# A fused recurrent-attention and MLP kernel: the second-layer weights loaded in fp32 by the common queue and cast on the chip, with the later order reworked

## The chip, the cores and the metric

The kernel runs on one core of one Trainium2 chip. The core has a matrix engine (TensorE, PE in the profile), a vector engine (VectorE, DVE), a scalar engine (ScalarE, ACT), a general engine (GpSimd, POOL) and SyncE (SP), which here only issues DMAs. Sixteen DMA engines move the data of all queues. The metric is the device time of one execution in microseconds, the median of several runs; lower is better.

## The reference

The inputs are r, k, v of shape (4, 8, 768, 48), that is batch, heads, time steps and head size, then w and u (8, 48), a norm's gain g_ln (384) and the weights w_ch1 (384, 1536) and w_ch2 (1536, 384), all in fp32.

```python
state = zeros(B, H, D, D)
for t in range(S):
    cur = einsum('bhd,bhe->bhde', u * k[t], v[t])
    y[t] = einsum('bhd,bhde->bhe', r[t], state + cur)
    state = w * state + einsum('bhd,bhe->bhde', k[t], v[t])
x = y as (B, S, H * D)
xn = (x - mean(x)) / sqrt(var(x) + 1e-6) * g_ln
out = x + maximum(xn @ w_ch1, 0) @ w_ch2
```

## The kernel before, in words

**Tiling.** The 4 x 768 time steps are cut into 24 chunks of 128 steps, six to a batch. Within a chunk the recurrence is done as matrix products: scaled k (`sk`) and scaled r (`sr`) are transposed, multiplied with each other and masked (`A`), and the sum of A times v and of the carried state `Z` times r is the chunk's y. Chunks 0 to 3 are worked on in another layout, with step names that end in 2. The MLP works on groups of chunks: chunks 0 to 7 and 20 to 23 are groups of one, chunks 8 to 19 are groups of two (`GROUPS`, line 14).

**Order.** The order is written out by hand in the string `PLAN` (lines 18 to 66). Each word is a step: its name, its index, and its engine (v VectorE, s ScalarE, g GpSimd, - for steps with one fixed engine, and for a DMA the queue of SP). The kernel issues the steps in that order (line 754), and each engine takes its own steps strictly in that order; semaphores make an engine wait where a step needs the result of another engine or a buffer that is still read. So a step that waits holds back everything behind it on its engine, and a DMA that waits on SP holds back all later DMAs of SP.

**Steps.** These are the ones that matter here; i is a chunk, g a pair of chunks.

- `LK`, `LR`, `LV` and `LK2`, `LR2`, `LV2` load k, r, v on SP (lines 350 to 376). They read pieces of 48 fp32 numbers.
- `LW1,kc` loads a third of w_ch1 (128 rows of 1536 fp32) into the tile `w1_f[kc]`. `SW,i` multiplies a 128 x 512 piece of it by the gain and casts it to bf16, into `w1_sb[n][kc]` with n = i // 3 and kc = i % 3.
- `IW2,n` loads a third of w_ch2 by a DMA on GpSimd's queue that casts from fp32 to bf16 as it moves the data, into `w2_sb[n]` (line 348).
- `SK`, `SR`, `SR2` scale k and r; `TRk`, `TRr` transpose them on TensorE, `TCk`, `TCr` copy the result out of PSUM; from chunk 8 on (for r from chunk 18 on) `TDk`, `TDr` do both by a transposing DMA on SP. `Q2` multiplies the transposed k and r; `AT`, `AT2` are the products, `AM`, `AM2` the masks.
- `CV2,g` casts the v of two chunks to bf16. `S,i` adds the outer products of chunk i to the state in PSUM, and for an even i first forms the diagonal terms, which `CC2` copies out and `VB2` multiplies by v. `ZU` and `ZD` finish the state.
- `Y,i` and `Y2,i` are y in PSUM; `X,i` adds the `VB2` part and gives x with its row sum; `SQ` is the sum of squares, `RS` the reciprocal root, `XN` the centred x in bf16. `LT` and `XT` transpose xn by TensorE and a copy; from group 8 on `LTD` does it by a transposing DMA on SP.
- `UP,16*g+m` is a piece of the first layer for group g (512 hidden columns in 12 matmuls for a group of one, 256 in 6 wider ones for a group of two), into one of two PSUM buffers that `Y2` uses as well; `RL` applies the maximum with 0 and frees that buffer. m runs over 0 to 2 for a group of one, and then needs the `SW` with n = m.
- `DN,4*i+d` is a third of the second layer for chunk i, reading `w2_sb[d]`. `OT,i` scales by `RS` and adds x, `STO` stores. `DU` are matmuls on zeros without use for the result.

The names that the profile prints are those of the program, with the digits of buffers left out: `w_sb` stands for the tiles of both weights, `hp` for the two PSUM buffers of `UP` and `Y2`, `y` for that of `S` and `Y`, `o` for that of `DN`, `at` for that of transposes and `AT`.

Of the kernel before, what the change touches and what calls it, by code (L numbers as in the profile page):

```python
# [29 lines left out]
DN,2,- Q2,3,g CV2,3,g RS,0,g S,6,- CC2,3,s RS,2,g RL,48,s VB2,3,g UP,50,- OT,0,v LR2,5,- LR2,6,- LK,8,- LK,9,- LK,12,- LK,11,-  # L30
LK,10,- SR2,5,g SK,9,g SR2,4,v ZU,6,v AM,6,v DN,4,- LT,4,- DN,5,- DN,6,- XT,4,s RL,50,s UP,49,- OT,1,v SK,8,v LT,5,- TRr,4,-
UP,65,- TCr,4,v XT,5,s RL,49,s RL,65,s RS,4,g SK,12,g SQ,3,s RS,3,s DN,8,- Y,6,- X,6,v XN,6,v DN,9,- DN,10,- S,7,- LT,6,-
UP,66,- OT,2,v ZU,7,v SR2,6,v DN,12,- Y,7,- DN,13,- DN,14,- RL,66,v OT,3,v XT,6,s UP,82,- RL,82,s UP,64,- TDk,4,- LV,8,- LV,9,-
LK,13,- AT,8,- AT,9,- RS,5,g ZD,7,g Q2,4,g SK,11,g STO,0,- STO,2,- LV,13,- LR2,7,- LV,10,- SK,10,v TDk,5,- LV,11,- X,7,v RL,64,s
CV2,4,s XN,7,s AM,8,v AM,9,v UP,98,- UP,97,- DN,16,- RL,98,s UP,80,- S,8,- DN,17,- TRr,5,- ZU,8,v SK,13,g CC2,4,s RL,97,s SQ,6,s
DN,18,- S,9,- LT,7,- RL,80,s OT,4,v ZD,8,v ZU,9,v VB2,4,g UP,81,- RL,81,v XT,7,s TCr,5,s DN,20,- TRr,6,- Y,9,- UP,96,- Q2,5,v
X,9,v STO,1,- LK,17,- LK,16,- TDk,6,- UP,113,- Y,8,- DN,21,- DN,22,- X,8,v ZD,9,v XN,8,v XN,9,g TCr,6,s CV2,5,s SQ,8,s S,10,-
ZU,10,v ZD,10,g SK,17,v OT,5,v CC2,5,v RL,113,s RL,96,s SQ,7,s AT,10,- AT,11,- UP,114,- UP,112,- SR2,7,v AM,11,v VB2,5,g RS,6,g
RS,7,g SK,16,g DN,24,- DN,25,- DN,26,- RL,112,s RL,114,s AM,10,v Y,11,- X,11,v OT,6,v LTD,8,- UP,133,- UP,128,- RL,133,v STO,3,-
LV,14,- LK,14,- LV,12,- LK,15,- LR2,8,- LR,18,- AT,13,- AT,12,- Y,10,- Q2,6,v X,10,v RL,128,s SQ,9,s RS,8,g AM,12,v SK,14,v  # L40
DN,28,- UP,129,- UP,131,- DN,29,- XN,10,s XN,11,s RL,129,s RL,131,s CV2,6,g DN,30,- S,12,- UP,130,- UP,132,- AM,13,v OT,7,v
SK,15,v LTD,9,- LV,15,- TDk,7,- STO,4,- LR,19,- STO,5,- LK,19,- CC2,6,s RL,130,s RL,132,s DN,32,- TRr,7,- ZU,12,v Y,13,- VB2,6,v
X,13,v XN,13,g UP,146,- DN,33,- TCr,7,v RL,146,s Y,12,- UP,144,- CV2,7,v UP,148,- DN,34,- RL,148,s RL,144,s SQ,11,s X,12,v
S,13,- Q2,7,v OT,8,v XN,12,g SR2,8,g AT,14,- AT,15,- UP,149,- DN,36,- LTD,10,- LV,16,- LV,17,- TDk,8,- LR,21,- LK,18,- LK,20,-
STO,7,- STO,6,- ZU,13,v ZD,13,v S,14,- AM,15,v SQ,12,s RL,149,s DN,37,- DN,38,- UP,147,- SQ,13,s SQ,10,s CC2,7,v ZU,14,v
RL,147,s ZD,14,g AM,14,v VB2,7,g SR,18,g SK,19,g UP,161,- S,15,- ZU,15,v RL,161,s TRr,8,- UP,163,- UP,145,- RL,163,s TCr,8,s
CV2,8,s RS,9,g Y,15,- OT,9,v RL,145,v X,15,v UP,164,- UP,160,- Y,14,- X,14,v XN,14,g SK,18,g ZD,15,g SR,19,v Q2,8,v DN,44,-
AT,17,- AT,16,- XN,15,s RL,160,s RL,164,s LTD,11,- UP,162,- DN,45,- DN,46,- S,16,- RL,162,s CC2,8,s SQ,15,s RS,10,s AM,16,v
OT,11,v LV,18,- TDk,9,- TDr,9,- STO,8,- UP,165,- ZU,16,v VB2,8,v DN,40,- DN,41,- DN,42,- RL,165,s SQ,14,s RS,11,s LV,19,-
SK,20,g Q2,9,g OT,10,v ZD,16,v Y,16,- UP,180,- RL,180,s AM,17,v X,16,v XN,16,v DN,48,- UP,177,- DN,49,- UP,176,- DN,50,-  # L50
RL,176,s Y,17,- OT,12,v AT,19,- AT,18,- X,17,v UP,178,- DN,52,- XN,17,s CV2,9,v AM,18,v S,18,- DN,53,- SQ,17,s CC2,9,s RL,178,s
RL,177,s VB2,9,g DN,54,- ZU,18,v STO,9,- LR,20,- OT,13,v SR,20,g SR,21,g LK,21,- STO,12,- LTD,12,- STO,11,- STO,10,- UP,179,-
RL,179,s Y,18,- UP,181,- DN,56,- DN,57,- UP,194,- AM,19,v RL,181,v DN,58,- X,18,v UP,193,- Y,19,- LV,20,- LV,21,- TDr,10,-
OT,14,v X,19,v XN,18,v XN,19,v SQ,18,s RL,193,s RL,194,v DN,60,- UP,197,- S,19,- DN,61,- UP,192,- SQ,16,s RS,12,s RL,197,s
SQ,19,s ZU,19,v CV2,10,v RL,192,v SK,21,g TDk,10,- Q2,10,g DN,62,- UP,195,- UP,196,- RL,195,s RL,196,s OT,15,v ZD,19,v AT,21,-
AT,20,- AM,20,v AM,21,v LTD,13,- LK,23,- LK,22,- LR,22,- LR,23,- SK,23,g SK,22,g SR,22,g STO,13,- TDk,11,- STO,14,- SR,23,g
TDr,11,- Q2,11,g DN,64,- DN,65,- UP,208,- S,20,- UP,210,- DN,66,- ZU,20,v RL,208,s CC2,10,s RL,210,s UP,212,- Y,20,- RL,212,s
OT,16,v UP,209,- DN,68,- DN,69,- VB2,10,v X,20,v RL,209,v ZD,20,v UP,213,- DN,70,- OT,17,v UP,211,- Y,21,- RS,13,s XN,20,s
RL,213,s RL,211,s LV,22,- LTD,14,- LV,23,- DN,72,- DN,73,- AT,23,- AT,22,- X,21,v S,21,- DN,74,- AM,23,v ZU,21,v OT,18,v
CV2,11,g UP,224,- UP,225,- DN,76,- SQ,21,s XN,21,s SQ,20,s RL,225,s LTD,15,- STO,16,- STO,15,- S,22,- ZD,21,g AM,22,v CC2,11,v  # L60
ZU,22,v VB2,11,g UP,240,- DN,77,- RL,240,s RS,15,s RL,224,s Y,22,- DN,78,- UP,242,- UP,226,- X,22,v ZD,22,v OT,19,v XN,22,s
RS,14,g RL,226,s RL,242,v DN,80,- Y,23,- X,23,v DN,81,- DN,82,- UP,241,- LTD,16,- UP,257,- OT,20,v RL,241,s RL,257,s DN,84,-
# [724 lines left out]
```

## Time and profile before

| | us |
|---|---|
| median of 3 runs | 153.11 (152.23 to 153.35) |
| the profiled execution | 151.87 |
| its span, first to last instruction | 150.1 |
| TensorE busy, of the span | 140.2 (93%) |
| VectorE, ScalarE, GpSimd busy | 112.8, 82.3, 87.7 |

The profile is of one execution. A line such as `L650 PE MATMUL hp<-xT,w_sb ... x648 | 57.7, 240 | 0.5 <-DVE` says: line 650, on TensorE, matmuls that read xT and w_sb and write hp, 648 of them, 57.7 us busy in all, 240 ns for one on average, and 0.5 us in which TensorE had waited ahead of them for VectorE. A row of the waits such as `PE y L485 <- POOL vv L394: 2.7, 1, 2.7` gives the engine that waited with its line, the one it waited for, us in total, how often, and the longest. Matmuls overlap, so the time of one step is better read from the chain of waits, where rows follow each other in time (start, length, what). SPq and POOLq are the issuing of DMAs.

### The profile page before, as it was taken

To read this page: it belongs to the slowest core of one execution; us is meant where nothing else is said; L and a number is where in the kernel's file an instruction comes from. 1 tells how busy PE (TensorE), PEld (TensorE's weight loads), DVE (VectorE), ACT (ScalarE), POOL (GpSimd) and SP (SyncE) were. 2 spreads that over 40 slices of the span, in tenths; PEclk is the share of its full clock that TensorE was granted. 3 is DMA by queue.
4 is the path that set the end of the run, shared out by engine and by line. 5 is a ranking of instruction groups with operands and counts; after the bars stand their busy time and mean duration, and the time that the engine had idled before them with its cause. 6 is when DMAs were issued, how large, how long until landed. Compare 5 with 4: busy or idle time off the path is not lost.

```text
span 150.1 us, 4669 instructions
## 1 busy us (share of the span) xinstructions
PE 140.2 (93%) x1936; PEld 112.4 (75%) x1936; DVE 112.8 (75%) x195; ACT 82.3 (55%) x181; POOL 87.7 (58%) x107
## 2 busy tenths in 40 slices
PE   7998798669999899999999999999999999999991
...
GB/s 117 298 240 327 258 364 223 223 236 207 186 129 24 213 216 215 168 129 177 231 146 202 160 213 168 142 207 207 210 162 177 190 155 161 135 24 38 158 144 66
DMA packets 84329, 27.18 MB, mean 181 GB/s; under 512 B 80338, under 2 KB 83540, under 8 KB 84308
## 3 DMA queue, kind: packets, MB, share of 16 engines
...
q10 hardware_dynamic: 2, 0.00, 0.0%
...
## 4 chain that ended last, share of the span: by engine, by line
PE 68%; SPq 12%; DMA 10%; POOL 4%; DVE 2%; issue 1%; ACT 0%; POOLq 0%; ACTq 0%
PE hp L650 29%; PE o L678 25%; DMA vf<-in_v_dram 7%; SPq L334 3%; DMA xT<-xn 3%; PE at L548 3%; SPq L351 2%; PE y L587 2%; SPq L373 2%; PE y L485 2%; SPq L376 2%; PE y L579 2%; POOL Vb L496 1%; POOL sr L204 1%; PE at L404 1%; SPq L370 1%
## 5 line engine op out<-in xcount | busy, mean ns | idle before, releaser
L650 PE MATMUL hp<-xT,w_sb 128*128 128x128 bf16 (+1 forms) x648 | 57.7, 240 | 0.5 <-DVE w_sb L343 0.4
L650 PEld LDWEIGHTS <-w_sb 128*128 128x128 bf16 x648 | 49.8, 115 | 4.2 <-DVE w_sb L343 0.5
L678 PE MATMUL o<-w_sb,hT 128*128 128x384 bf16 x276 | 52.8, 326 | 0.0
L666 ACT ACTIVATE hT<-hp 128x512 bf16<-128x512 f32 x55 | 32.1, 596 | 35.6 <-PE hp L650 35.0
L678 PEld LDWEIGHTS <-hT 128*128 128x128 bf16 x276 | 25.1, 98 | 11.9
L557 DVE TENSOR_TENSOR A<-at,mask 128x1024 bf16<-128x1024 f32 x20 | 24.0, 1213 | 1.1 <-PE at L548 1.1
L734 DVE SCALAR_TENSOR_TENSOR ot<-o,rs,x 128x384 f32<-128x384 f32 x23 | 14.1, 614 | 9.3 <-PE o L678 7.5
L496 POOL TENSOR_TENSOR Vb<-vf,cc 128x768 f32<-128x768 f32 x9 | 14.8, 1642 | 6.7 <-ACT cc L199 6.0
L204 POOL TENSOR_TENSOR q<-trk,trr 128x1024 bf16<-128x1024 bf16 x5 | 10.7, 2131 | 13.6 <-DMA trk<-sk 4.9
L204 POOL TENSOR_TENSOR sk<-kf,Fk 128x384 bf16<-128x384 f32 (+1 forms) x15 | 16.4, 1103 | 0.9 <-DMA kf<-in_k_dram 0.9
L204 POOL TENSOR_TENSOR sr<-rf,Fr 128x384 bf16<-128x384 f32 (+1 forms) x11 | 16.1, 1477 | 1.1 <-ACT Fr L297 1.0
L594 DVE SCALAR_TENSOR_TENSOR x<-y,Vb 128x384 f32<-128x384 f32 x20 | 11.0, 551 | 7.3 <-PE y L587 6.0
L601 ACT ACTIVATE sqj<-x,sm 128x384 bf16<-128x384 f32 x24 | 14.7, 610 | 3.4 <-DVE x L594 3.2
L668 DVE TENSOR_SCALAR hT<-hp 128x512 bf16<-128x512 f32 x17 | 11.5, 685 | 3.9 <-PE hp L650 3.9
L610 POOL TENSOR_SCALAR xn<-x,sm 128x384 bf16<-128x384 f32 x8 | 5.7, 716 | 12.3 <-DVE x L594 12.1
L485 PE MATMUL y<-vv,sk 128*128 128x96 bf16 (+1 forms) x96 | 7.5, 207 | 2.7 <-POOL vv L394 2.7
L204 POOL TENSOR_TENSOR Z<-ZS,WLZ 128x384 bf16<-128x384 f32 x5 | 5.9, 1183 | 5.0 <-DVE ZS L569 5.0
L278 PE MATMUL o<-warm 128*128 128x512 bf16 x26 | 7.7, 437 | 1.0 <-DVE warm L227 1.0
L485 PEld LDWEIGHTS <-sk 128*128 128x128 bf16 (+1 forms) x96 | 5.3, 97 | 4.3 <-issue 3.7
L204 DVE TENSOR_TENSOR sk<-kf,Fk 128x384 bf16<-128x384 f32 x8 | 5.9, 752 | 3.1 <-ACT Fk L300 3.1
L199 ACT COPY trr<-at 128x512 bf16<-128x512 bf16 (+1 forms) x11 | 7.7, 774 | 0.4 <-PE at L404 0.4
L620 POOL TENSOR_SCALAR rs<-sq 128x1 f32<-128x1 f32 (+1 forms) x10 | 1.9, 193 | 10.2 <-ACT sqj L601 9.6
...
## 6 DMA issues: line engine op xcount, KB each, us to landing
out_dram<-ot SPq DMA_DIRECT2D x23, 192.0 KB, 3.3
kf<-in_k_dram SPq DMA_DIRECT2D x20, 192.0 KB, 4.7
vf<-in_v_dram SPq DMA_DIRECT2D x20, 192.0 KB, 3.7
rf<-in_r_dram SPq DMA_DIRECT2D x9, 384.0 KB, 4.6
w_f<-in_moe_w_ch_dram SPq DMA_DIRECT2D x3, 768.0 KB, 6.9
w_sb<-in_moe_w_ch_dram POOLq DMA_DIRECT2D x3, 384.0 KB, 6.9
rf<-in_r_dram SPq DMA_DIRECT2D x6, 192.0 KB, 3.5
kf<-in_k_dram SPq DMA_DIRECT2D x2, 384.0 KB, 4.4
```

The source lines that it names most:

```text
L199: nc.scalar.copy(out=out, in_=in_)
L204: engines[e].tensor_tensor(out=out, in0=in0, in1=in1, op=ALU.mult)
L485: nc.tensor.matmul(out=t[:, q * E2 : (q + 1) * E2].rearrange("p (e d) -> p e d", e=2), lhsT=lhs, rhs=rhs, start=first, stop=True, skip_gro ...
L496: engines[e].tensor_tensor(out=Vb2(g).rearrange("p (x h d) -> p x h d", x=2, h=H), in0=vals, in1=cc2(g)[:].unsqueeze(3).to_broadcast([P, 2 ...
L557: nc.vector.tensor_tensor(out=AA(i)[:].rearrange("p e q t -> p (e q) t"), in0=psum["at", i][:].rearrange("p e q t -> p (e q) t"), in1=mask ...
L594: nc.vector.scalar_tensor_tensor(out=xx(i)[:], in0=psum["y", i][:, :C], scalar=1.0, in1=Vb(i), op0=ALU.mult, op1=ALU.add, accum_out=sm[i][:],)
L601: nc.scalar.activation(out=sqj[:], in_=xx(i)[:], func=ACT.Square, bias=sm[i][:], scale=-float(C), accum_out=sq[g][:, j : j + 1])
L650: nc.tensor.matmul(out=t[:, a * gw : (a + 1) * gw], lhsT=w1_sb[n][kc][:, fb::FB], rhs=xT(g)[:, :size, kc, :], start=(kc == 0), stop=(kc == ...
L666: nc.scalar.activation(out=o, in_=s, func=ACT.Relu)
L668: nc.vector.tensor_relu(out=o, in_=s)
L678: nc.tensor.matmul(out=psum["o", i][:, :C], lhsT=hT(g)[:, fk, j * P : (j + 1) * P], rhs=w2_sb[d][:, a, :], start=(fk == 0), stop=(fk == FK ...
L734: nc.vector.scalar_tensor_tensor(out=ot(i)[:], in0=psum["o", i][:, :C], scalar=rs[g][:, j : j + 1], in1=xx(i)[:], op0=ALU.mult, op1=ALU.add,)
```

## The change

The three casting loads `IW2` on GpSimd's queue are gone. `LW2,n` on SP's queue reads the same third of w_ch2 as fp32 into `w1_f[n]`, the tile that held a third of w_ch1; so it must wait until `SW` n, n + 3 and n + 6 have read that tile. Six steps `CW2,i` cast half a third each (128 x 768) to bf16, three on GpSimd (0, 2 and 5) and three on ScalarE (1, 3 and 4); `w2_sb` is cut into halves accordingly, and `DN` picks the half. The three fp32 tiles get another name, nothing else changes in them. `LW2` stands in the order behind `LV,4` and `LV,5`, ahead of `LV,7`, `LV,6` and all later loads.

From line 23 on the order of the steps is another one, and 106 steps that are in both versions run on another engine. Among them, `SW` stands four times on GpSimd, four times on ScalarE and once on VectorE (before: two, six and one), `XN` twelve times on GpSimd (before: eight), `Q2` always on VectorE (before: five of twelve on GpSimd). The matmuls are the same.

```diff
--- before
+++ after
@@ the order, from line 23 @@
-SR2,3,g VB2,0,g SR2,2,g AT2,1,- TRk,1,- S,1,- FR,0,s TCk,1,s CV2,1,s UGC,0,s AM2,1,v Y2,1,- TRr,3,- Y2,0,- Q2,1,v TCr,3,s ZU,1,v
-X,0,v AT2,3,- LK,6,- LV,5,- LV,4,- S,2,- AM2,3,v ZU,2,v AT2,2,- AM2,2,v SW,6,s CC2,1,s XN,0,g MP,4,g SK,5,g TRr,2,- TCr,2,s
-VB2,1,g SW,3,g IW2,0,g IW2,1,g SK,7,g DU,1024,- S,3,- X,1,v XN,1,v TRk,2,- TCk,2,s LT,0,- Y2,2,- AT,4,- XT,0,v X,2,v AM,4,v
-SW,2,g SW,8,v LR2,4,- LV,6,- LV,7,- SW,7,s SW,1,s SW,4,s AT,5,- Y2,3,- DU,512,- LT,1,- UP,2,- X,3,v CV2,2,g SK,6,v XN,3,g XN,2,g
-IW2,2,g SW,5,s RL,2,v XT,1,s UP,17,- SQ,0,s SW,0,s RL,17,s Q2,2,v ZU,3,v TRk,3,- UP,0,- UP,18,- S,4,- AM,5,v TCk,3,s RL,0,s
-UP,16,- LT,2,- RL,18,v LT,3,- UP,1,- CC2,2,s RL,16,s XT,2,v UP,33,- RL,33,s SQ,1,s RL,1,s VB2,2,g ZU,4,v XT,3,v Y,5,- X,5,v
-DN,0,- UP,34,- Y,4,- X,4,v RL,34,v UP,32,- AT,7,- AT,6,- RS,1,s SQ,4,s SQ,2,s SQ,5,s XN,4,s RL,32,v XN,5,v AM,7,v DN,1,- UP,48,-
...
+SR2,3,g VB2,0,g AT2,1,- TRk,1,- S,1,- FR,0,s TCk,1,s AM2,1,v Y2,1,- LK,6,- LV,4,- LV,5,- TRr,3,- Y2,0,- TCr,3,s CV2,1,g ZU,1,v
+Q2,1,v X,1,v SR2,2,v AT2,3,- S,2,- AM2,3,v TRr,2,- SQ,1,s TCr,2,s CC2,1,v ZU,2,v X,0,v AT2,2,- DU,1024,- S,3,- AM2,2,v MP,4,g
+XN,1,g SK,5,g VB2,1,g TRk,2,- XN,0,s LT,0,- UGC,0,s SW,6,s XT,0,s ZU,3,v TCk,2,v Y2,2,- LT,1,- AT,4,- Y2,3,- X,2,v AM,4,v SW,8,v
+SW,7,s XT,1,s SW,3,s SW,4,s SK,7,g SW,0,g XN,2,g DU,512,- AT,5,- LT,2,- UP,2,- SW,5,g SW,2,g SW,1,g X,3,v XN,3,v XT,2,v RL,2,s
+UP,18,- LT,3,- SK,6,v XT,3,v Q2,2,v AM,5,v RL,18,s UP,1,- TRk,3,- UP,0,- RL,1,s TCk,3,s RL,0,v UP,50,- SQ,0,s LW2,0,- CV2,2,g
+S,4,- CC2,2,s VB2,2,g CW2,0,g UP,48,- CW2,1,s RL,50,s RL,48,s LW2,2,- CW2,5,g AT,6,- AT,7,- ZU,4,v Y,5,- X,5,v XN,5,v AM,6,v
+UP,33,- UP,16,- SQ,2,s RL,16,s RL,33,s LW2,1,- LV,7,- LV,6,- CW2,3,s CW2,4,s LK,9,- LK,11,- LR2,4,- LR2,5,- LK,8,- LV,9,-
+LR2,6,- LV,10,- Y,4,- CW2,2,g DN,0,- UP,32,- UP,17,- RL,32,s DN,1,- DN,2,- CV2,3,g RS,0,s Q2,3,v X,4,v LT,5,- AM,7,v OT,0,v
+SR2,4,g RS,2,g XN,4,g S,6,- UP,49,- RS,1,s CC2,3,s RL,17,v VB2,3,v SQ,4,s XT,5,s DN,4,- UP,80,- RL,80,s SQ,3,s RL,49,s DN,5,-
+DN,6,- ZU,6,v SK,9,v UP,81,- RL,81,v OT,1,v UP,34,- TRr,4,- Y,7,- RL,34,v X,7,v RS,4,s TCr,4,s DN,8,- LT,4,- XT,4,s DN,9,-
+DN,10,- S,7,- UP,65,- SK,8,g TDk,4,- LV,8,- LK,10,- LK,14,- LV,13,- LR2,7,- STO,0,- LV,11,- ZU,7,v OT,2,v SR2,5,g TRr,5,-
...
+Y,9,- DN,18,- TRr,6,- VB2,4,g UP,113,- AM,8,v X,9,v OT,4,v S,9,- ZU,9,v LT,6,- DN,20,- Y,8,- DN,21,- UP,112,- DN,22,- X,8,v
+XT,6,v XN,9,g SR2,7,g TDk,5,- LV,16,- CV2,5,g XN,8,g RL,113,s SQ,5,s TCr,6,s SQ,9,s RS,5,s Q2,5,v RL,112,s UP,97,- RL,97,s
+AT,11,- AT,10,- UP,96,- STO,1,- STO,2,- LK,13,- OT,5,v LK,12,- SK,13,g LTD,8,- LK,15,- LV,12,- UP,114,- S,10,- ZD,9,v SK,12,v
+TDk,6,- AM,11,v ZU,10,v CC2,5,v ZD,10,v RL,96,s UP,98,- DN,24,- SQ,6,s RL,114,s RL,98,s RS,6,s UP,131,- AM,10,v RL,131,v
...
@@ -185,9 +185,9 @@
     g_neg = const.tile([P, CK], FP32, name="g_neg")
     WLZ = const.tile([P, HP, E2], FP32, name="WLZ")
     uwI = const.tile([P, HP, 2], BF16, name="uwI")
-    w1_f = [const.tile([P, F], FP32, name=f"w1_f{kc}") for kc in range(CK)]
+    w1_f = [const.tile([P, F], FP32, name=f"w_f{kc}") for kc in range(CK)]
     w1_sb = [[const.tile([P, FW], BF16, name=f"w1_sb{n}_{kc}") for kc in range(CK)] for n in range(NW)]
-    w2_sb = [const.tile([P, FK // NW, C], BF16, name=f"w2_sb{n}") for n in range(NW)]
+    w2_sb = [[const.tile([P, FB // 2, C], BF16, name=f"w2_sb{n}_{a}") for a in range(2)] for n in range(NW)]
     w1_src = moe_w_ch1.rearrange("(kc p) f -> p kc f", p=P)
     w2_src = moe_w_ch2.rearrange("(n p fk) c -> p n fk c", p=P, n=NW)
 
@@ -344,8 +344,16 @@
         else:
             nc.gpsimd.tensor_scalar(out=o, in0=s, scalar1=g, scalar2=1.0, op0=ALU.mult, op1=ALU.mult)
 
-    def IW2(n, e):
-        nc.gpsimd.dma_start(out=w2_sb[n][:], in_=w2_src[:, n])
+    def LW2(n, e):
+        queues[e].dma_start(out=w1_f[n][:].rearrange("p (k c) -> p k c", k=FB), in_=w2_src[:, n])
+
+    def CW2(i, e):
+        n, a = divmod(i, 2)
+        o, s = w2_sb[n][a][:].rearrange("p k c -> p (k c)"), w1_f[n][:, a * F // 2 : (a + 1) * F // 2]
+        if e == "g":
+            nc.gpsimd.tensor_scalar(out=o, in0=s, scalar1=1.0, scalar2=1.0, op0=ALU.mult, op1=ALU.mult)
+        else:
+            copy(e, o, s)
 
     def LK(i, e):
         queues[e].dma_start(out=kf(i), in_=chunk_src(k, i))
@@ -678,7 +686,7 @@
             nc.tensor.matmul(
                 out=psum["o", i][:, :C],
                 lhsT=hT(g)[:, fk, j * P : (j + 1) * P],
-                rhs=w2_sb[d][:, a, :],
+                rhs=w2_sb[d][2 * a // FB][:, a % (FB // 2), :],
                 start=(fk == 0),
                 stop=(fk == FK - 1),
             )
@@ -693,7 +701,7 @@
             nc.tensor.matmul(
                 out=psum[name][:, : C // 2],
                 lhsT=hT(g)[:, fk, j * P : (j + 1) * P],
-                rhs=w2_sb[i][:, a, c0 : c0 + C // 2],
+                rhs=w2_sb[i][2 * a // FB][:, a % (FB // 2), c0 : c0 + C // 2],
                 start=(fk == 0),
                 stop=(fk == FK - 1),
             )
@@ -745,7 +753,7 @@
 
     steps = dict(
         MW=MW, MO=MO, ML=ML, MZ=MZ, MI=MI, MI2=MI2, MM=MM, MM2=MM2, MP=MP, TL=TL, DU=DU, WF=WF, UF=UF, LG=LG, UGC=UGC,
-        LN=LN, WBM=WBM, FK=FK_, FR=FR_, FK2=FK2, FR2=FR2, UWR=UWR, COL=COL, UW=UW, WL=WL, LW1=LW1, SW=SW, IW2=IW2,
+        LN=LN, WBM=WBM, FK=FK_, FR=FR_, FK2=FK2, FR2=FR2, UWR=UWR, COL=COL, UW=UW, WL=WL, LW1=LW1, SW=SW, LW2=LW2, CW2=CW2,
         LK=LK, LR=LR, LV=LV, LK2=LK2, LR2=LR2, LV2=LV2, SK=SK, SR=SR, SK2=SK2, SR2=SR2, SKH=SKH, SRH=SRH, CV2=CV2,
         TRk=TRk, TRr=TRr, TCk=TCk, TCr=TCr, TDk=TDk, TDr=TDr, Q2=Q2, AT2=AT2, AT=AT, AM2=AM2, AM=AM, S=S_, CC2=CC2,
         ZU=ZU, ZD=ZD, VB2=VB2, Y2=Y2, Y=Y, X=X, SQ=SQ, XN=XN, RS=RS, LT=LT, LTD=LTD, XT=XT, UP=UP, RL=RL, DN=DN,
```

64 lines of the change are left out of this document (28 added, 36 removed).

## The prediction

> **What bounds the kernel now.** I read the page first (shares, and the span in 40 slices), then PE's own waits, then busy times by stretch, then the chain of waits back from the stall.
>
> ```profile
> PE 140.2 (93%) x1936; PEld 112.4 (75%) x1936; DVE 112.8 (75%) x195; ACT 82.3 (55%) x181; POOL 87.7 (58%) x107
> ...
> PE   7998798669999899999999999999999999999991
> ```
>
> TensorE is busy for 93% of the span, and its missing 9.9 us lie almost wholly in the first 14 slices and the last. Its waits, from 28 us on:
>
> ```profile
> PE y L485 <- POOL vv L394: 2.7, 1, 2.7
> PE at L635 <- DVE xn L610: 0.7, 1, 0.7
> ```
>
> The busy times by stretch (length, then busy us with count of PE, PEld, DVE, ACT, POOL; then granted clock, DMA share, GB/s):
>
> ```profile
> 28.75:31.51 2.76, 0.01 (x2) 0.00 (x1) 0.74 (x2) 0.00 (x0) 0.89 (x2) 0.95 1.16 270
> 31.25:34.66 3.41, 3.15 (x32) 3.15 (x31) 1.04 (x3) 0.77 (x2) 3.38 (x6) 0.50 0.98 212
> ```
>
> ```profile
> 65.00:70.00 5.00, 4.85 (x71) 3.79 (x69) 4.78 (x7) 2.57 (x6) 3.97 (x4) 1.00 0.61 130
> ...
> 80.00:100.00 20.00, 20.00 (x238) 16.48 (x235) 17.08 (x29) 13.32 (x32) 12.16 (x13) 1.00 0.89 191
> 100.00:120.00 20.00, 20.00 (x221) 16.08 (x220) 17.15 (x28) 9.39 (x23) 11.87 (x10) 1.00 0.97 186
> ```
>
> Late in the kernel TensorE never pauses, so only fewer matmuls or an earlier start help there. The one large hole is 28.75 to 31.51, behind which the granted clock stands at 0.50 for 3.41 us. The chain of waits (start, us) says who made the hole:
>
> ```profile
> 20.10 10.37 DMA vf<-in_v_dram
> ...
> 30.62 0.84 POOL vv L394
> ...
> 31.51 0.48 PE y L485 x4
> ...
> 36.03 0.65 PE o L678 x4
> 36.69 0.67 PE hp L650 x12
> ...
> 41.04 0.18 PE y L464 x8
> ```
>
> The second v load of chunks 4 and 5 is issued at 20.10 and lands 10.37 us later; GpSimd casts it (CV2,2), and only then can S,4 go on. (The rows at 36 us are one DN, 0.65, and one UP, 0.67; S,6 begins at 41.04.) The issues around it:
>
> ```profile
> 19.42 4.19 SPq L357 DMA_DIRECT2D vf<-in_v_dram  x2
> 22.47 1.34 POOL L348 DMA_DIRECT2D w_sb<-in_moe_w_ch_dram  x2
> ```
>
> ```profile
> w_sb<-in_moe_w_ch_dram POOLq DMA_DIRECT2D x1, 384.0 KB, 5.3
> vf<-in_v_dram SPq DMA_DIRECT2D x1, 192.0 KB, 10.4
> ```
>
> (The second pair is the DMA view for 22.4 to 23.2 us, the last number being us to landing.) The first casting weight load starts at 22.47, over 2 us after that v load, and is down at about 27.8, 2.7 us before it. So the weight loads on GpSimd's queue pass the v load that the next matmul needs.
>
> **The change, part by part.**
>
> *The weight loads move (IW2 gone, three LW2 in).* LW2 stands on SP's queue behind LV,4 and LV,5, so it cannot pass them. Without the overtaking I give the second load twice the usual landing:
>
> ```profile
> w_f<-in_moe_w_ch_dram SPq DMA_DIRECT2D x3, 768.0 KB, 6.9
> ...
> xT<-xn SPq DMA_TRANSPOSE x10, 2.8
> ```
>
> ```profile
> L357 SPq DMA_DIRECT2D vf<-in_v_dram x20: 428/610/3505, 19.4 to 125.1; - x20
> ...
> DMA to landing us min/median/max: 3.1/3.7/10.4
> ```
>
> 20.10 + 7.4 = 27.5. CV2,2 costs GpSimd 0.83 (below) and S,4 now has five UP ahead of it, so the stall goes: 2.75 us. The half clock behind it goes too: 3.15 us of work done at clock 0.50 is 1.6 us lost. Together -4.35. What GpSimd spent on issuing (three times about 0.6) goes as well, off the path.
>
> *The order before the first UP.* In the old order UP,2 waits for SW,8 on VectorE (its row of the timeline, then groups of VectorE by shape: xn, Z, sr, three copies):
>
> ```profile
> 24.24 0.89 DVE L343 TENSOR_SCALAR w_sb<-w_f,g_neg 128x512 bf16<-128x512 f32 x1
> ```
>
> ```profile
> L610 DVE TENSOR_SCALAR xn<-x,sm 128x384 bf16<-128x384 f32 x7 | 5.7, 832 | 0.1
> ...
> L204 DVE TENSOR_TENSOR Z<-y,WLZ 128x384 bf16<-128x384 f32 x8 | 4.4, 547 | 0.8 <-PE y L485 0.8
> ...
> L204 DVE TENSOR_TENSOR sr<-rf,Fr 128x768 bf16<-128x768 f32 x3 | 3.1, 1021 | 0.0
> ...
> L201 DVE COPY xT<-at 128x384 bf16<-128x384 bf16 x3 | 1.1, 350 | 4.1 <-PE at L635 4.1
> ...
> L201 DVE COPY trr<-at 128x1024 bf16<-128x1024 bf16 x1 | 0.7, 692 | 0.5 <-PE at L404 0.5
> ...
> L201 DVE COPY cc<-y 128x16 f32<-128x16 f32 x3 | 0.5, 165 | 0.2 <-PE y L485 0.2
> ```
>
> Between Q2,1 and SW,8 VectorE gains SR2,2 (1.02), ZU,3 (0.55), TCk,2 (0.69) and CC2,1 (0.17), and loses ZU,1 (0.55, now ahead of Q2,1), XN,1 (0.83) and XT,0 (0.35): 2.43 - 1.73 = +0.70. With 0.1 for its waits on x, SW,8 ends at about 25.9, not 25.1, and I charge +0.8. Bounds: 0, if VectorE's old small waits absorb it; +1.8, if SR2,2 doubles beside GpSimd.
>
> *SP's new waits.* LW2,n overwrites the fp32 W1 tile n, so SP waits for SW n, n+3 and n+6. Four SW are now on GpSimd, and there XN,2 waits for X,2 (VectorE, about 24.0), then come SW,5, SW,2, SW,1 (groups by shape, and the Vb rows' shortest, median and longest):
>
> ```profile
> L666 ACT ACTIVATE hT<-hp 128x512 bf16<-128x512 f32 x55 | 32.1, 596 | 35.6 <-PE hp L650 35.0
> ...
> L610 POOL TENSOR_SCALAR xn<-x,sm 128x384 bf16<-128x384 f32 x8 | 5.7, 716 | 12.3 <-DVE x L594 12.1
> ...
> L199 ACT CAST vv<-vf 128x768 bf16<-128x768 f32 x5 | 4.2, 838 | 1.0 <-DMA vf<-in_v_dram 1.0
> ...
> L341 ACT ACTIVATE w_sb<-w_f,g_neg 128x512 bf16<-128x512 f32 x6 | 4.0, 715 | 0.0
> ...
> L394 POOL TENSOR_SCALAR vv<-vf 128x768 bf16<-128x768 f32 x4 | 3.3, 831 | 5.8 <-DMA vf<-in_v_dram 5.7
> ...
> L345 POOL TENSOR_SCALAR w_sb<-w_f,g_neg 128x512 bf16<-128x512 f32 x2 | 1.7, 835 | 0.0
> ```
>
> ```profile
> L496 POOL TENSOR_TENSOR Vb<-vf,cc x9: 1476/1480/2228, 14.7 to 130.8; 128x768 f32<-128x768 f32 x9
> ```
>
> 24.0 + 0.72 + 3 x 0.835 = 27.2 for SW,1. X,2 stands one mask step ahead of SW,8, hence 24.0. LW2,0 can go when ScalarE has done SW,3 (about 24.9: X,0 at 21.0, then XN,0, three SW at 0.715 and two XT), LW2,2 at 26.4, LW2,1 at 27.2. By the W1 loads' 6.9 us they land at 31.8, 33.3 and 34.1. Queued behind them on SP are LV,7, LV,6 and all later loads: issued by about 29.3, landed by 33 (3.7) to 36.7 (the last weight load's 34.1 and one v load's worth more). Their reader CV2,3 comes on GpSimd after the casts, at 35.2, and S,6 wants it at 37.8: hidden, up to +0.5 at the bad end.
>
> *Six casts.* Three on ScalarE at 0.838, three on GpSimd at 0.831, same shape as CV2. TensorE: UP,2 from 25.95, five UP at 0.67, LT,3 and TRk,3 0.8 (S,4 at 30.1, until 30.85), then UP,48, AT,6, AT,7 and Y,5 1.6, UP,33 at 32.45, UP,16, Y,4, and DN,0 at 34.2, DN,1 at 36.2. GpSimd: CC2,2 follows S,4 at about 31.1, then VB2,2 1.48 (32.6), CW2,0 (33.5), CW2,5 (34.3), CW2,2 (35.2): 0.7 ahead of DN,0 and 1.0 ahead of DN,1, covered by S,4, UP and Y. Without cover, all four steps longer by half (2228 against 1476), the chain ends at 37.1 and costs 0.95. On ScalarE CW2,1 stands behind CC2,2, and behind it RL,50, which frees the PSUM buffer for UP,33: with LW2,0 down by 31.1 it is 31.15 + 0.84 + 0.6 = 32.6, 0.15 late; with LW2,0 at 31.8 it is 33.25, 0.8 late. The queue is nearly empty by then, so I stay near the early end: +0.4. CW2,3 and CW2,4 end at 35.8, before DN,1 and DN,2.
>
> The row says that a GpSimd step on the same operands takes 1.48 or 2.23 us. [...]
>
> *Later order.* Same matmuls; the steps are reshuffled from line 23 on, and 106 of them stand on another engine. TensorE has no slack to win beyond the 0.7 above. Bounds 0 to about 6 (rival three); I take +0.4, near the old trace, which shows no pause after 80 us.
>
> *Sum.* Without the PSUM wait S,6 begins at 34.2 + three DN + two UP + LT,5 = 37.8, not 41.04, with one LT more done: -3.55, which is -4.35 + 0.8. With 0.4 for RL,50 and 0.4 for the later order: -2.75. The profiled execution took 151.87 with a span of 150.1; I expect 149.1 and 147.35. The median shown is 153.11, 1.24 above the profiled one; the same gain gives **150.4**.
>
> **Rivals.**
>
> *One: GpSimd stretched*, as priced: -2.75 + 0.95, 151.3. For: 2.23 in the Vb row. [...] Chance 0.15.
>
> *Two: the v load lands no earlier.* SP needed 3.5 us to issue it, and DMA share was 1.16 in the hole: had the engines merely been full, the queue would not matter. The hole and the half clock stay, VectorE's 0.8 comes on top: 153.9. Against: the weight load that passed. Chance 0.08. [...]
>
> *Three, on the slow side: late xT transposes.* From chunk 8 on, each UP group waits on x, xn, one transposing DMA.
>
> ```profile
> 64.58 0.34 DVE xn L610
> 65.07 4.55 DMA xT<-xn
> 69.67 1.50 PE hp L650 x12
> ```
>
> Already TensorE waits a little for the first (0.15 of the 5 us to 70). The new order puts XN,8 on GpSimd behind SR2,7 and CV2,5, and twelve XN on GpSimd, not eight. With ten transposes, 0.6 us of waiting at each costs 6.0: -3.15 + 6.0 is 156.0. It decides for slower at 4.7 in all, 0.47 each. Half of it, 0.3 each, gives 153.0. Against: in the old order SP itself waited often for its operands and TensorE stayed full from 80 to 120. Chance 0.16 for the whole, 0.13 for the half.
>
> **How the numbers follow.** The plain forecast keeps 0.48. One per cent (1.5 us) is about what a measurement here can tell from nothing. Faster (under 151.6): forecast and rival one, 0.63. Within: rival two and the half of three, 0.21. Slower: 0.16. The forecast's own span is 148.0 (nothing lost before UP,2 or later, 0.15 for RL,50, and the median 0.9 nearer the profiled execution) to 152.3 (SR2,2 doubled, RL,50 at 0.8, CV2,3 at 0.5). The range takes in all cases but the whole of three, 0.84 less thin tails: 148.0 to 153.9.
>
> **What would show it.** In the new trace: no wait of TensorE on vv around 30 us and no half clock there; vf of chunks 4 and 5 landed by 27.5; S,6 near 38.2; CW2 near 0.83 each on both engines, with no wait of DN (L678 of the old numbering) on w_sb; SP waiting at LW2 until 25 to 27 us. I am wrong if TensorE waits more than 1 us in all for casts, for SW or for vv, if a half clock shows up again, or if waits for xT add up to over 1.5 us after 60 us.

## The result and the profile after

The changed kernel took 151.45 us (median of 20 runs, 150.73 to 154.62), the one before 153.19 beside it (20 runs, 152.04 to 154.88). The ratio is 0.9897, with a 95% interval of 0.9871 to 0.9924: 1.0% faster, 1.74 us between the medians. A ratio leaves out executions that took over 1.5% more than the quickest of their kernel on that chip; by which old ones those are, ratios from different chips can differ by some 0.3%. The forecast was 150.4, in a range of 148.0 to 153.9, so the direction and the range held and the gain came out at two thirds of what was forecast.

The two profiled executions are closer together than the medians: 151.51 against 151.87 in all, spans of 149.7 and 150.1. The old one was quicker than each of the 20 old runs. Its granted clock over the span is 0.989, which is one stretch of 3.41 us at 0.50; of 23 old executions that ran later beside the changed kernel nine show 0.989 (median 152.78) and eight show 0.978 (median 154.65), as two such stretches would give; five of the other six stand at 0.933 or 0.955, one at 1.00. Of the changed kernel's 20, 18 show 0.997 to 1.00.

No old execution with 0.978 was profiled, but two kernels of the experiments below, which keep the old order up to there, show a half clock early in their profiles. The first row is of the old order with the casting loads later; the loads alone have 0.50 from 19.7 to 23.1. It comes behind a hole of TensorE of 0.65 us. The second row is of the old kernel's own profile, which has the same hole, 0.64, with the clock at 1.00 behind it:

```profile
19.30:22.70 3.40, 3.35 (x35) 2.17 (x34) 3.04 (x5) 2.11 (x4) 3.08 (x5) 0.50 0.85 254
```

```profile
18.85 0.44 PE L447 MATMUL at<-trr,trk 48*64 48x128 bf16 x16 [0.64 <-DVE A L529]
```

So the old order loses a half clock there in some executions. In none of the ten profiles of the new order does the clock fall there.

The page, engine shares and TensorE's 40 slices:

```profile
PE 141.3 (94%) x1936; PEld 111.1 (74%) x1936; DVE 106.7 (71%) x191; ACT 83.5 (56%) x180; POOL 89.6 (60%) x115
...
PE   7998989998999799999999999999999999999991
```

The 6 of the eighth and ninth slice is gone; VectorE has 6 us less to do, GpSimd 2 more. TensorE's own waits (engine, line, waited for, us in total, times, longest):

```profile
PE y L472 <- DVE x L602: 0.9, 1, 0.9
...
PE at L412 <- POOL sr L204: 0.5, 2, 0.3
...
PE o L686 <- POOL w_sb L354: 0.4, 1, 0.4
```

No wait on vv is left. The three rows are new, and all of them hang on something that SP loaded late. By stretch:

```profile
25.00:30.00 5.00, 4.95 (x94) 4.77 (x94) 4.96 (x11) 3.39 (x7) 2.75 (x4) 1.00 0.83 261
26.40:28.00 1.60, 1.60 (x32) 1.60 (x31) 1.60 (x5) 1.24 (x3) 1.28 (x2) 1.00 0.61 164
30.00:35.00 5.00, 4.83 (x95) 4.30 (x93) 3.51 (x7) 3.63 (x9) 3.08 (x3) 1.00 1.00 332
34.00:36.00 2.00, 1.97 (x28) 1.67 (x27) 2.00 (x3) 1.43 (x3) 0.65 (x1) 1.00 0.54 108
...
50.00:55.00 5.00, 3.98 (x60) 2.97 (x59) 4.21 (x9) 2.51 (x6) 2.46 (x2) 1.00 1.25 241
...
80.00:100.00 20.00, 20.00 (x232) 16.43 (x231) 16.81 (x29) 10.72 (x26) 12.02 (x14) 1.00 1.09 207
```

The clock is 1.00 where it was 0.50. The DMA share falls to 0.61 and 0.54 in two short stretches of the phase in which loads decide, and a new hole of TensorE has opened at 50 to 55. SP's queue and GpSimd's rows show its way (start, us, line, what, and in brackets the idle time ahead and what ended it):

```profile
18.69 5.53 SPq L365 DMA_DIRECT2D vf<-in_v_dram  x2
24.62 2.66 SPq L348 DMA_DIRECT2D w_f<-in_moe_w_ch_dram  x3
27.33 2.21 SPq L365 DMA_DIRECT2D vf<-in_v_dram  x2
29.58 6.09 SPq L359 DMA_DIRECT2D kf<-in_k_dram  x2
35.72 1.70 SPq L381 DMA_DIRECT2D rf<-in_r_dram  x2
...
46.17 1.33 SPq L435 DMA_TRANSPOSE trk<-sk  x1
```

```profile
27.25 0.83 POOL L402 TENSOR_SCALAR vv<-vf 128x768 bf16<-128x768 f32 x1 [0.32 <-DMA vf<-in_v_dram]
30.59 1.48 POOL L504 TENSOR_TENSOR Vb<-vf,cc 128x768 f32<-128x768 f32 x1 [2.51 <-ACT cc L199]
32.04 1.63 POOL L354 TENSOR_SCALAR w_sb<-w_f 128x768 bf16<-128x768 f32 x2
35.35 0.95 POOL L354 TENSOR_SCALAR w_sb<-w_f 128x768 bf16<-128x768 f32 x1 [1.68 <-DMA w_f<-in_moe_w_ch_dram]
...
41.73 1.83 POOL L204 TENSOR_TENSOR sr<-rf,Fr 128x768 bf16<-128x768 f32 x1 [4.18 <-DMA rf<-in_r_dram]
```

The r of chunks 8 and 9 (LR2,4) was issued at 23.73 in the old trace. Now it is issued at 35.72, behind three weight loads, two v and two k loads. Its reader SR2,4 waits 4.18 us on GpSimd and runs at 41.73; SK,8 stands behind it on GpSimd, TDk,4 (46.17) needs SK,8, and Q2,4 (VectorE waits 2.62 us ahead of it for the transposed k), X,6 and S,8 follow, where the 0.9 us of waiting for x stands. The profile's own chain reaches `sk` by another way, over the cast of the last weight load, TensorE and VectorE:

```profile
26.95 8.33 DMA w_f<-in_moe_w_ch_dram
35.35 0.96 POOL w_sb L354
...
43.88 0.69 DVE hT L676
44.57 0.02 issue
44.59 0.59 POOL xn L618
45.18 0.97 POOL sk L204
46.17 1.33 SPq L435
```

But XN,4, the xn here, begins 0.12 us behind GpSimd's step ahead of it, as it does in the new order with old casting loads (43.32 to 43.44), where no hT ends just then. So from SR2,4 to SK,8 GpSimd is held up by nothing else, and the late r decides when TDk,4 goes.

How much was won and given back can be read from two steps of TensorE, S,6 and the last group of the second layer. Of the kernel before, then of the changed one:

```profile
40.88 0.34 PE L464 MATMUL y<-uwI,q 128*128 128x2 bf16 x8
...
146.18 0.82 PE L693 MATMUL o<-w_sb,hT 128*128 128x192 bf16 x8
```

```profile
37.82 0.34 PE L472 MATMUL y<-uwI,q 128*128 128x2 bf16 x8
...
145.75 0.82 PE L701 MATMUL o<-w_sb,hT 128*128 128x192 bf16 x8
```

S,6 begins 3.06 us earlier, with one LT more already done. From there to the end of the last group the old kernel takes 147.00 - 40.88 = 106.12 us, the new one 146.57 - 37.82 = 108.75. Of 3.06 won ahead of S,6, 2.63 are lost behind it.

### The profile page after: what moved, and what is told of

It is laid out like the page before. It is cut to its first block, busy times and chain, and to the rows that moved or that the text cites. A ratio compares the mean times of both kernels' runs of the same rounds, so it can differ in the third digit from the quotient of the medians.

```text
span 149.7 us, 4680 instructions
## 1 busy us (share of the span) xinstructions
PE 141.3 (94%) x1936; PEld 111.1 (74%) x1936; DVE 106.7 (71%) x191; ACT 83.5 (56%) x180; POOL 89.6 (60%) x115
## 4 chain that ended last, share of the span: by engine, by line
PE 58%; DMA 11%; POOL 11%; ACT 5%; DVE 5%; SPq 4%; issue 4%; DVEq 0%; ACTq 0%; POOLq 0%
PE o L686 22%; PE hp L658 20%; DMA w_f<-in_moe_w_ch_dram 6%; DMA vf<-in_v_dram 3%; PE o L278 3%; DMA rf<-in_r_dram 3%; POOL sr L204 2%; PE at L412 2%; POOL Vb L504 2%; PE y L493 2%; PE at L556 2%; SPq L359 2%; POOL xn L618 2%; POOL w_sb L345 2%; PE y L595 2%
## 5 line engine op out<-in xcount | busy, mean ns | idle before, releaser
L658 PE MATMUL hp<-xT,w_sb 128*128 128x128 bf16 (+1 forms) x648 | 56.1, 237 | 0.6 <-ACT hT L674 0.2
L686 PE MATMUL o<-w_sb,hT 128*128 128x384 bf16 x276 | 51.7, 326 | 0.4 <-POOL w_sb L354 0.4
L204 POOL TENSOR_TENSOR sr<-rf,Fr 128x768 bf16<-128x768 f32 (+1 forms) x12 | 18.4, 1535 | 5.9 <-DMA rf<-in_r_dram 4.5
L204 POOL TENSOR_TENSOR Z<-ZS,WLZ 128x384 bf16<-128x384 f32 x7 | 7.7, 1097 | 11.0 <-DVE ZS L577 11.0
L618 POOL TENSOR_SCALAR xn<-x,sm 128x384 bf16<-128x384 f32 x12 | 8.8, 730 | 8.7 <-DVE x L602 8.4
L204 DVE TENSOR_TENSOR q<-trk,trr 128x1024 bf16<-128x1024 bf16 x12 | 10.6, 880 | 3.4 <-DMA trk<-sk 3.2
L199 ACT COPY trr<-at 128x512 bf16<-128x512 bf16 (+1 forms) x15 | 10.3, 757 | 3.6 <-PE at L412 2.2
L577 DVE TENSOR_TENSOR ZS<-y,Z 128x384 f32<-128x384 f32 x12 | 6.6, 553 | 2.2 <-PE y L493 2.2
L616 ACT ACTIVATE xn<-x,sm 128x384 bf16<-128x384 f32 x9 | 5.5, 614 | 4.3 <-POOL xn L618 2.2
L631 POOL TENSOR_TENSOR rs<-rs,expo 128x2 f32<-128x2 f32 (+1 forms) x11 | 7.2, 651 | 0.9
```

The source lines that it names most:

```text
L204: engines[e].tensor_tensor(out=out, in0=in0, in1=in1, op=ALU.mult)
L618: engines[e].tensor_scalar(out=xn(g)[:, j], in0=xx(i)[:], scalar1=-float(C), scalar2=sm[i][:], op0=ALU.mult, op1=ALU.add)
L658: nc.tensor.matmul(out=t[:, a * gw : (a + 1) * gw], lhsT=w1_sb[n][kc][:, fb::FB], rhs=xT(g)[:, :size, kc, :], start=(kc == 0), stop=(kc == ...
L686: nc.tensor.matmul(out=psum["o", i][:, :C], lhsT=hT(g)[:, fk, j * P : (j + 1) * P], rhs=w2_sb[d][2 * a // FB][:, a % (FB // 2), :], start= ...
```

## The experiments

Two questions. What made the v load late in the old kernel: the casting loads on GpSimd's queue, which pass it (theory Q), or DMA engines that are merely full (F)? And what gives back the gain behind S,6: r, k and v loads that come late because they stand in one line behind the weights (L), or the reworked order of the engines (O)? Ratios are to the kernel before on the same chip, with 95% intervals. Line numbers are one lower than in the kernel that each is made from, except for the loads alone and the unaltered changed kernel.

### The casting loads later, in the old order

```diff
-VB2,1,g SW,3,g IW2,0,g IW2,1,g SK,7,g
+VB2,1,g SW,3,g SK,7,g
...
-CV2,2,g
+CV2,2,g IW2,0,g IW2,1,g
```

> The old kernel with one edit: the first two casting weight loads stand behind CV2,2 on GpSimd, so they are issued only when the v of chunks 4 and 5 is down. Theory Q (the casting loads pass the v load): v lands near 25.5 to 27, the hole before S,4 and the half clock go, 3 to 4 us faster than before, less what DN,0 waits if the weights come after 33. Theory F (the DMA engines were merely full): v lands near 30 as before, no faster than before by more than 0.5 us.

Measured: 151.95, ratio 0.9852 (0.9783 to 0.992). GpSimd's row of CV2,2, then TensorE's of DN,0:

```profile
29.04 0.83 POOL L393 TENSOR_SCALAR vv<-vf 128x768 bf16<-128x768 f32 x1 [2.49 <-DMA vf<-in_v_dram]
```

```profile
36.43 0.81 PE L677 MATMUL o<-w_sb,hT 128*128 128x384 bf16 x4 [1.81 <-DMA w_sb<-in_moe_w_ch_dram]
```

With no load on GpSimd's queue ahead of it the v is cast at 29.04, not 30.62. SP issued it later here (21.62, not 20.10), so the time to landing says more. From the chain:

```profile
21.62 7.27 DMA vf<-in_v_dram
```

It is 7.27 us, not 10.37: Q holds, for 3.1 us. The other 3.6 above the median of 3.7 are there without casting loads; that full engines cause them (F) is not shown apart from SP's own line. And the weights, asked for later, are late for DN,0 by 1.81 us.

### The hole filled with matmuls without use

```diff
-S,4,-
+DU,6144,- S,4,-
```

> The old kernel with twelve matmuls on zeros put ahead of S,4, so that TensorE is busy while it waits for v. If the half clock behind the hole costs the 1.6 us that I charged, this is 1.3 to 1.9 us faster than before, though it adds work. If the half clock costs nothing that lasts, it is the same as before or up to 0.5 us slower.

Measured: 152.24, ratio 0.9865 (0.979 to 0.9941). TensorE's busy time around the old half clock, then its rows of S,4 and S,6:

```profile
30.00:35.00 5.00, 4.00 (x54) 2.90 (x52) 0.81 (x3) 0.77 (x2) 3.19 (x5) 1.00 1.02 232
```

```profile
32.67 0.33 PE L484 MATMUL y<-vv,sk 128*128 128x96 bf16 x4 [0.86 <-POOL vv L393]
...
40.87 0.34 PE L463 MATMUL y<-uwI,q 128*128 128x2 bf16 x8
```

The v came no earlier (its cast begins at 31.78) and matmuls were added, yet the clock stayed at 1.00 and the median is 2.1 us lower. The profiles give the half clock alone: from S,4 to S,6 it takes 8.20 us here and 9.37 in the old kernel (31.51 to 40.88), so it is worth 1.2, somewhat less than the 1.6 that the prediction charged. The 2.1 of the medians holds more than that: three of the seven old executions beside this one have clocks of 0.933 and 0.955, which one such stretch does not explain.

### The new order with the old casting loads

Against the changed kernel, with `IW2` and `w_sb` as before:

```diff
-SW,4,s SK,7,g
+SW,4,s IW2,0,g IW2,1,g SK,7,g
...
-SQ,0,s LW2,0,- CV2,2,g
+SQ,0,s CV2,2,g IW2,2,g
...
-VB2,2,g CW2,0,g UP,48,- CW2,1,s RL,50,s RL,48,s LW2,2,- CW2,5,g AT,6,-
+VB2,2,g UP,48,- RL,50,s RL,48,s AT,6,-
...
-RL,33,s LW2,1,- LV,7,- LV,6,- CW2,3,s CW2,4,s LK,9,-
+RL,33,s LV,7,- LV,6,- LK,9,-
...
-Y,4,- CW2,2,g DN,0,-
+Y,4,- DN,0,-
```

> The new order with the old casting loads on GpSimd, as early as in the old kernel (two ahead of SK,7, one behind CV2,2). Theory Q: the v load is passed again, lands near 30, S,4 waits about 1 us or more (it now has five UP ahead), and the time lies 0.5 to 2.5 us above the changed kernel, about that of the kernel before. Theory F: it is as fast as the changed kernel or a little faster, for the six casts are gone.

> The new order with the old casting loads once more, on the same chip as the three above. If the order alone carries the gain of the change, it lies 1 to 2 per cent below before, and within 0.7 us of the changed kernel (151.5).

Run on two chips: 150.96, ratio 0.9782 (0.9712 to 0.9852), and 150.57, ratio 0.9796 (0.9741 to 0.9851). GpSimd, then TensorE of the first:

```profile
31.78 0.83 POOL L393 TENSOR_SCALAR vv<-vf 128x768 bf16<-128x768 f32 x1 [3.72 <-DMA vf<-in_v_dram]
...
39.97 1.83 POOL L203 TENSOR_TENSOR sr<-rf,Fr 128x768 bf16<-128x768 f32 x1 [4.34 <-DMA rf<-in_r_dram]
```

```profile
39.71 0.34 PE L463 MATMUL y<-uwI,q 128*128 128x2 bf16 x8
...
144.54 0.82 PE L692 MATMUL o<-w_sb,hT 128*128 128x192 bf16 x8
```

The v load is late again, later than in the old kernel, as Q says. But the time does not follow, and the forecast by Q, slower than the changed kernel by 0.5 to 2.5 us, is wrong: this half of the change came out faster than the whole, by 0.5 to 1.1 us of the medians. The two were never run on one chip, but the changed kernel took 151.45 and 151.69 on two, and neither interval overlaps that of the whole (0.9871 to 0.9924). Five UP stand ahead of S,4 in the new order (four in the old), so TensorE waits 1.6 and 1.8 us there, not 2.75, and the clock stays at 1.00 behind it. From S,6 on it takes 105.65 us, in the second profile 105.66. The old order takes 106.12, so the reworked order by itself gives nothing back: O falls.

### The new order with the casting loads late

Against the kernel just shown:

```diff
-SW,4,s IW2,0,g IW2,1,g SK,7,g
+SW,4,s SK,7,g
...
-CV2,2,g IW2,2,g
+CV2,2,g IW2,0,g IW2,1,g IW2,2,g
```

> The new order with casting loads on GpSimd, all three issued behind CV2,2, when the v of chunks 4 and 5 is down. No casts, no wait of SP for the W1 tiles. Theory L, in the form that the second run of e3 suggests (the changed kernel starves its later loads, for SP waits for SW ahead of LW2 and everything stands in one line behind 2.3 MB of weights): no hole at S,4, the r load of chunks 8 and 9 lands well ahead of 41.7, where the changed kernel has it, and the time is 0.5 to 2 us below the changed kernel, unless DN,0 waits for weights that come after 34. Theory O: the same as the changed kernel within 0.5 us.

Measured: 151.13, ratio 0.9878 (0.9837 to 0.992). TensorE's row of DN,0, then two stretches behind it:

```profile
36.43 0.81 PE L677 MATMUL o<-w_sb,hT 128*128 128x384 bf16 x4 [2.11 <-DMA w_sb<-in_moe_w_ch_dram]
```

```profile
37.00:40.40 3.40, 3.40 (x29) 2.98 (x28) 0.36 (x1) 1.37 (x5) 0.00 (x0) 0.52 1.09 237
```

The stall has only moved: from v to the weights, with a half clock of its own. The v is cast at 28.69, but the r of chunks 8 and 9 did not come well ahead of the change's, as was expected, though no weights stand in SP's line: SR2,4 begins at 40.94 after 7.18 us of waiting, in the change at 41.73 and 43.18. The time can't be told from the change's on that chip (0.9919, below). The DMA share is 1.04 from 30 to 35 us and 1.09 from 35 to 40. My reading is that the 16 engines have too much to bring by 36 us, and the order of issue decided here which reader paid: v, issued first, was cast in time at 28.69, and DN,0 waited 2.11 us for the weights.

### The loads alone, in the old order

`LW2` and `CW2` as in the changed kernel, but third n goes to the W1 tile (n + 1) mod 3, since the old order has its last reads of the three tiles in another sequence:

```diff
-VB2,1,g SW,3,g IW2,0,g IW2,1,g SK,7,g
+VB2,1,g SW,3,g SK,7,g
...
-SW,8,v LR2,4,- LV,6,- LV,7,- SW,7,s
+SW,8,v SW,7,s
...
-IW2,2,g SW,5,s RL,2,v
+SW,5,s LW2,0,- LW2,1,- LR2,4,- LV,6,- LV,7,- RL,2,v
...
-SW,0,s RL,17,s
+SW,0,s LW2,2,- RL,17,s
...
-CC2,2,s RL,16,s
+CC2,2,s CW2,1,s RL,16,s
...
-RL,1,s VB2,2,g
+RL,1,s CW2,3,s CW2,4,s VB2,2,g CW2,0,g CW2,2,g CW2,5,g
```

> The old order of the steps with only the weights changed as in the change: three fp32 loads on SP behind the v of chunks 4 and 5, into the used W1 tiles, and six casts on the same engines. If the gain of the change comes from the loads, this is 2 to 3 us faster than before. If it comes mostly from the order, this gains the hole (2.7) and the half clock (1.6) but pays for late loads and casts, and stays within 1.5 us of before.

Measured: 154.41, ratio 1.0041 (0.9997 to 1.0084). TensorE's waits and the third load on SP:

```profile
PE o L686 <- ACT w_sb L199: 1.8, 1, 1.8
PE y L472 <- POOL q L204: 1.3, 1, 1.3
```

```profile
32.53 1.06 SPq L348 DMA_DIRECT2D w_f<-in_moe_w_ch_dram  x1
```

The loads alone gain nothing, though the wait on the v of chunks 4 and 5 is gone. In the old order the last W1 tile is read for the last time so late that the third load goes at 32.53; DN then waits on its cast, the clock halves a second time (0.50 from 45 to 47, after the early stretch from 19.7), and TDk,4 slips to 49.39 (from 47.07). Without the new order the new loads do not pay; with the old loads the new order does.

### The changed kernel with one weight load

Left out are two of the three loads: all six casts read the third that is loaded, so two thirds of w_ch2 are wrong values, and two thirds of the weights' bytes are not moved.

```diff
-LW2,2,- ... LW2,1,-
...
-    w1_f[n][:, a * F // 2 : (a + 1) * F // 2]
+    w1_f[0][:, a * F // 2 : (a + 1) * F // 2]
```

> The changed kernel without two of the three weight loads; all six casts read the one that is left, so two thirds of the second layer's weights are wrong values, and about 4 us of transfer are gone from ahead of the later loads. Theory L (the gain is given back from 35 to 55 us because the r and k loads come late behind the weights): the waits of TensorE at the transposes of r (43 and 48 us) and at S,8 (0.9 us at 52) go, 1 to 2.3 us faster than the changed kernel. Theory O (it is given back by the reworked order on the engines): at most 0.4 us faster, which is the one wait for a cast at 36 us.

Measured: ratio 0.962 (0.9531 to 0.971), resting on two executions (147.77 and 148.66), a profiled span of 146.0. GpSimd, SP and TensorE:

```profile
36.45 1.81 POOL L203 TENSOR_TENSOR sr<-rf,Fr 128x768 bf16<-128x768 f32 x1
```

```profile
41.61 1.34 SPq L434 DMA_TRANSPOSE trk<-sk  x1
```

```profile
37.60 0.34 PE L471 MATMUL y<-uwI,q 128*128 128x2 bf16 x8
...
142.21 0.82 PE L700 MATMUL o<-w_sb,hT 128*128 128x192 bf16 x8
```

S,6 begins when it does in the changed kernel (37.60, 37.82). But SR2,4 waits for no load, TDk,4 goes 4.56 us earlier, and from S,6 to the end it takes 143.03 - 37.60 = 105.43, not 108.75. With the order of the steps untouched, the 2.6 us given back are gone: L holds. It does not tell the place in SP's line from the bytes, for both are less.

### The changed kernel again, and with r first

```diff
-LK,9,- LK,11,- LR2,4,- LR2,5,- LK,8,- LV,9,-
+LR2,4,- LK,8,- LK,9,- LK,11,- LR2,5,- LV,9,-
```

> The changed kernel itself, unaltered, on the same chip as the three others, so that they can be set beside it: 1.0 to 1.3 per cent below before.

> The changed kernel with two loads moved on SP: the r of chunks 8 and 9 and the k of chunk 8 ahead of the k of chunks 9 and 11. The same transfers in another order. Theory L: SR2,4 starts about 2 us sooner (its wait of 4.2 us shrinks), TDk,4 goes 1 to 2 us sooner, the wait at S,8 (0.9) goes; 0.4 to 1.2 us faster than the changed kernel. Theory O: no difference beyond 0.3 us.

On one chip the unaltered changed kernel took 151.69 (ratio 0.9919, 0.9877 to 0.9961), the one with r first 150.32 (0.9818, 0.9758 to 0.9878). TDk,4 on SP, of the unaltered kernel and of the other:

```profile
47.62 1.33 SPq L435 DMA_TRANSPOSE trk<-sk  x1
```

```profile
44.60 2.16 SPq L434 DMA_TRANSPOSE trk<-sk  x1
```

Two loads moved up in SP's line, no byte and no step of an engine changed, and 0.9% is back; the two intervals just touch. TDk,4 goes 3.0 us earlier, but from S,6 to the end only 1.1 are won (107.08, not 108.19): now the v of chunk 8 comes late, and TensorE waits 1.3 for its cast. In the second profile of the changed kernel the last weight load was later still: DN,1 waited 1.4 us for its cast (0.4 in the first profile), the v of chunks 4 and 5 was cast at 28.82, not 27.25, and S,6 began at 39.22.

### Versions that join the two

The new order with the old casting loads, and r, k and one v moved up on SP:

```diff
-LK,9,- LK,11,- LR2,4,- LR2,5,- LK,8,- LV,9,- LR2,6,-
+LR2,4,- LK,8,- LK,9,- LK,11,- LR2,5,- LV,9,- LV,8,- LR2,6,-
...
-TDk,4,- LV,8,- LK,10,-
+TDk,4,- LK,10,-
```

The same with one casting load early and two late:

```diff
-SW,4,s IW2,0,g IW2,1,g SK,7,g
+SW,4,s IW2,0,g SK,7,g
...
-CV2,2,g IW2,2,g
+CV2,2,g IW2,1,g IW2,2,g
```

The third is the changed kernel, with `LW2`, and the first of these two diffs.

> The new order with the old casting loads on GpSimd (two early, one behind CV2,2) and, on SP, the r of chunks 8 and 9 and the k of chunk 8 ahead of the k of chunks 9 and 11, and the v of chunk 8 ahead of two later loads. Theory L: a little below the new order with the old loads alone, 0.3 to 1 us, and 2.5 to 3.5 us below before. Theory O: equal to the new order with the old loads within 0.3 us.

> As the one before, but only the first casting load is early, two stand behind CV2,2. Theory Q: v is passed by one load, not by two, so it lands about 2 us sooner (near 29) and S,4 waits little; weights two and three land near 33 and 35, about when DN,1 and DN,2 want them. 2.5 to 4 us below before, and 0 to 1 us below the one before it.

> The changed kernel with the same moves on SP (r of chunks 8 and 9, k of chunk 8, v of chunk 8 earlier). Theory L: as with the first two moves alone, and the wait of 1.3 us that TensorE had there for the cast v of chunk 8 (near 52 us) goes too: 1 to 2 us faster than the changed kernel. Theory O: the same as the changed kernel within 0.5 us.

Ratios in this order: 0.9786 (0.971 to 0.9862), 0.9778 (0.9712 to 0.9845), 0.9794 (0.9739 to 0.9849). All three are about 2% below the kernel before and about 1% below the change, and none can be told from the others or from the new order with the old loads; the 0.3 to 1 us that the first was expected to gain over the latter did not show. Moving r up on top of the casting loads has added nothing that can be measured; on top of `LW2` it has.

The profiles side by side, all from the same rows of TensorE and SP: S,6, how far TDk,4 is behind it, and the time from S,6 to the end of the last group.

| kernel | S,6 | TDk,4 behind it | S,6 to the end |
|---|---|---|---|
| before | 40.88 | 6.19 | 106.12 |
| old order, casting loads later | 41.43 | 6.19 | 105.87 |
| old order, hole filled | 40.87 | 6.20 | 107.02 |
| old order, loads alone | 41.59 | 7.80 | 108.02 |
| the change, two profiles | 37.82, 39.22 | 8.35, 8.40 | 108.75, 108.19 |
| new order, old casting loads, two profiles | 39.71, 40.70 | 5.32, 5.33 | 105.65, 105.66 |
| new order, casting loads late | 41.53 | 4.61 | 105.30 |
| new order, casting loads, r, k and v up | 39.39 | 4.59 | 105.33 |
| the same, one casting load early | 40.30 | 4.78 | 105.83 |
| one weight load | 37.60 | 4.01 | 105.43 |
| r first | 39.24 | 5.36 | 107.08 |
| r and v first | 38.70 | 5.91 | 106.74 |

Loading the weights on SP wins 1.7 us up to S,6 over the same order with casting loads (the means of the two profiles) and loses 2.8 behind it. The last column scatters: the old order with its hole filled has the old kernel's steps behind S,6 and takes 0.9 more, 0.7 of it one wait for an xT.

The loss is not all a later r. From S,6 to S,8 TensorE takes 12.34 us with old casting loads in both profiles, and with one weight load; in the change it takes 14.66 and 14.54, so most of the 2.8 lies there. SR2,4 starts at 41.73 and 43.18 in the change, at 39.97 and 40.97 with the casting loads: r is about 2 us later. But S,8 came no less than 6.1 us behind TDk,4 in any profile. An estimate with the means of two profiles each: TensorE alone would have brought the change to S,8 at 50.9 (38.52 + 12.34); with TDk,4 as with the casting loads (45.53) S,8 could have come at 51.7, 6.2 later; it came at 53.1. So some 1.4 of the 2.3 us are r made later by the weights, and some 0.9 would have been lost anyway, as an earlier S,6 only meets the r and k loads sooner. Single profiles differ by 1 us and more, so the shares are rough.

## Why the prediction was right, and where it was not

**Right: the stall and the half clock.** No wait on vv, clock 1.00 from 30 to 35, and a v landed by 27.2 (27.5 forecast), though 28.8 in the second profile. That both went together was right; the cause was half right. With v as late as ever, the new order, which has five UP ahead of S,4, already avoids the half clock. Overtaking explains 3.1 us of the v load's 10.37 to landing in the old order and 3.6 in the new one (10.89, and 7.32 with the casting loads late). The landing orders agree (weights issued on GpSimd's queue at 22.47 down at about 27.8, the v issued on SP's at 20.10 at 30.47). On SP's own queue the first `LW2`, issued at 24.62 behind the v, came down behind it: at 30.0, 5.4 us later, the v by 27.2. By what mechanism a load on a second queue gets ahead isn't shown; no run here shows single packets. The half clock was charged at 1.6 and is worth 1.2 by the profile with the hole filled.

**Right: the first part of the sum.** UP,2 was expected at 25.95 and began at 25.57, as SW,8 took 0.60 on VectorE. SR2,2 took 1.10 there in the first profile, not twice 1.02 as at the slow end of the forecast's span. `LW2` went at 24.62 to 27.28 (24.9 to 27.2 forecast), DN,0 at 33.82 (34.2), DN,1 at 36.35 (36.2), S,6 at 37.98 in the chain's terms (37.8 to 38.2). Rival one did not occur: nothing of its 0.95 shows in the change, where VB2,2 took 1.48 and the casts 0.83 to 0.95. The 0.4 for RL,50 was not needed: UP,33 did not wait.

**Wrong: "Queued behind them on SP ... hidden, up to +0.5", and with it the later order's "+0.4, near the old trace".** The step named LV,7, LV,6 "and all later loads", but followed only the first reader, CV2,3, which was indeed hidden. The loads behind that one, the r and k of chunks 8 and 9, feed SR2,4, SK,8 and TDk,4. Between S,6 and the end 2.6 us were lost, 2.8 with the LT that is done earlier, where the sum had 0.4. That is the whole miss against the profiled execution (149.1 forecast, 151.51 measured). One weight load in place of three brings all of it back (105.43 from S,6 to the end), r ahead of k in the line 1.1 of it. So what stands ahead of r and k in SP's line costs time, and not the new order of the engines; and some 0.9, by the estimate above, is S,6 running ahead of the loads behind it, a limit that the sum did not have.

**Landing of the weights.** 31.8, 33.3, 34.1 were forecast with the 6.9 us of the W1 loads. The last took 8.33 and landed at 35.28. Its cast ended 1.1 us later than forecast, and the 1.0 of slack ahead of DN,1 became a wait of 0.4, in the second profile 1.4, which by the prediction's own sign (more than 1 us for casts) counts against it.

**Rival three did not occur.** After 60 us TensorE waits once for 0.2 (0.3 in the second profile), and not for an xT. The only late transpose that counted was TDk,4's. That such a wait occurs at all is seen in the old order with its hole filled, once, 0.7 us.

**The median: partly luck.** The profile-to-profile gain is 0.36 where 2.75 was forecast, the median's 1.74. The sum was made against an old execution with one half clock, and its gain was then set off from a median of executions that, by those run later, often have two. The new order is also free of the early stretch from about 19.5 us, for which the sum has no term. That made up for some of the 2.4 us that were missed, and so the median forecast was off by 1.05 only.

What stays open: why SP's issuing of two k loads took 6.09 us from 29.58 while the DMA share was 0.54 from 34 to 36; so how the later r divides between waiting for the W1 tiles, issuing, and moving bytes isn't settled. Nor is it shown which of the many reshuffled steps keeps the early clock at 1.00.
